# Two linear-attention layers and two memory-attention layers: stacking DMAs at slots 2 and 4, low parts taken at once, the output weight in four parts, the outer segments of the attention loop dealt anew

## The chip, the cores and the metric

The kernel runs on one core of a Trainium2 chip. The metric is the device time of one execution in microseconds. Three runs of the kernel before took 1543.25, 1537.27 and 1541.24 us, a median of 1541.24.

## What is computed

Four layers follow each other on x of 2048 tokens by 512 features, 32 heads of 16: A, B, A, B, each on a layer norm of x and added to x. A is linear attention with a learned feature map, B is causal softmax attention inside four segments of 512 tokens, mixed with a memory that sums over the segments before. The two A layers share their weights, and so do the two B layers.

```python
def _A_ref(x, wqkv, w_phi, wo):
    q, k, v = heads(x @ wqkv)
    pq, pk = q @ w_phi, k @ w_phi                      # per head
    phi = lambda p: concat([softmax(p), softmax(-p)])
    kv, z = sum_s phi(pk)^T v, sum_s phi(pk)
    return (phi(pq) @ kv / (phi(pq) @ z + 1e-6)) @ wo

def _B_ref(x, wq, wk, wv, wo, beta):
    g = sigmoid(beta)                                  # per head
    for s in range(4):                                 # segments of 512 tokens
        p = softmax(qs @ ks^T * 16**-0.5 + causal_mask)
        a_dot = p @ vs
        a_mem = phi(qs) @ M / (phi(qs) @ z + 1e-6)     # phi(t) = t + 1 if t > 0 else exp(t)
        o = g * a_mem + (1 - g) * a_dot
        M, z = M + phi(ks)^T vs, z + sum(phi(ks))
    return o @ wo

x = x + _A_ref(layernorm(x), ...); x = x + _B_ref(layernorm(x), ...)
x = x + _A_ref(layernorm(x), ...); x = x + _B_ref(layernorm(x), ...)
```

## The kernel before

Each float32 product of the projections is done as three float32r products: of an operand a high part (a copy rounded by ScalarE) and a low part (what is left, by VectorE) are made, and high x high, high x low and low x high are summed in PSUM (`mm3`, line 432). `mm3_pair` (line 447) does two such sums at once, each on one half of the rows of the array; they swap halves twice on the way, and the order at a swap is kept by a no-op on SyncE's queue (lines 458 to 462), between the last product before the swap and the first one after it.

The order of the work is written out by hand. TensorE, VectorE, ScalarE, GpSimd and SyncE each run their instructions in the order in which the program issues them (`held`, line 166; `Ordered`, line 146). All DMAs but one kind go through SyncE's queue.

The change concerns `LayerB.steps` (line 1291), the attention loop of a B layer. It has 32 units, one for each segment s (0 to 3) and each group m of four heads (eight to a segment), and five slots to a unit; k counts the slots, R = 5. In each slot the loop issues, in this order:

- one fifth of `attend` (line 1150): scores of a group into the PSUM tile `lg` (one buffer), ScalarE's exponential into `P`, GpSimd's causal mask
- one fifth of `maxima` (line 1105), which runs LEAD = 9 slots ahead: scores for the row maxima, into the PSUM tiles `mx` and `my` or, at slots 2 and 4, into two of the four `g` banks, and VectorE's masked maximum of each
- what was put off or set for this slot: `later`, `late`, and the parts and features of a projection (`projected`, line 1019: copies and splits into `ta`, features into `tb`)
- at slot STACK = 3: `stack` (line 1094), six DMAs that lay high and low parts of Q and K of a group side by side in a set `e` (`e<-ta`), for the group three units on
- at slot 0: `weighted` (line 1186), the weighted sum with the values of the unit before (`g<-P,v`), and ScalarE's scaled copy `U`
- the slot's entry in a table of text (lines 55 to 94): FIRST for segment 0, GAPS for segments 1 and 2, LAST and FINAL for segment 3 of the first and the second B layer

In the tables, "2.3" is slot 3 of unit 2 of the segment, and the words are taken from left to right by `do` (line 1305):

- `Qi/6`, `V/6`, `O/6`, `P/4`: so many steps of a pair of projections of queries and keys, of values, of the output, of the output of the last segment; a pair has 24 steps of two matmuls, so four cells of 6 make one; a + stands for the next segment
- `max`: `put_maxima` (line 1141), a transpose of the row maxima `mxs`, ScalarE's copy `mt` and a DMA from ScalarE's queue into Q's set (`e<-mt`)
- `fin`: `finish` (line 1209), four transposes of U, VectorE's division, the sum
- `ln`: one block of 128 tokens of the next segment's norm is transposed and split (`columns`, line 383); `turn` and `pt`: the same for a block of the attention's output (`turn`, line 472)
- `a0` to `a3`: half of a read of the memory (`reads`); `t0`, `m0` and so on: the transpose and the product of a write to it (`writes`)
- `n`, `N`, `load`, `begin`: a step of a norm (loads of x, moments); `w`: the load of the output weight `bwo` (`load_w`, line 224, eight DMAs of 256 KB)
- a `~` behind a word puts the low part, or the end, of that step off until after `attend` and `maxima` of the next slot (`wait`, line 133; `put_off`)

A unit without Q, V, O, v or P in its cells has no projection: units 2 and 3 of FIRST, 4, 5 and 6 of FINAL (6 has only row loads, `pre`). `opening` (line 1276) and the table BEFORE fill the slots ahead of unit 0, which run beside the last blocks of layer A.

## Time and profile before

| | |
|---|---|
| median of three runs | 1541.24 us |
| the profiled execution | 1534.9 us |
| its span, first to last instruction | 1533.1 us |
| mean granted TensorE clock | 0.974 |
| busy: TensorE, VectorE, ScalarE, GpSimd | 92%, 69%, 53%, 45% |
| first attention loop, from the first weighted sum after unit 0 to the last | 329.4 to 778.2 us |
| second attention loop, likewise | 1079.6 to 1517.9 us |

The page of the profile gives busy time, its shares in 40 slices, the DMA queues, the chain of work that ended last and the costliest groups of instructions. Other views give busy time by stretch, the instructions in order of time, and who waited for whom. PE is TensorE (PEld its weight loads), DVE VectorE, ACT ScalarE, POOL GpSimd, SP SyncE; a q behind an engine is its queue's own instructions, DMA issues among them. `g<-P,v` reads: written is tile g, read are tiles P and v. In a row of instructions stand start and length in us, engine, line, operation, tiles, shapes, count, and in brackets the engine's idle time before it with what ended it. Nearly all instructions are issued by two helpers (lines 156 and 178), so tiles tell more than lines.

### The profile page before, as it was taken

Reading aid. Unit: us, or ns where it says so; the run is one execution under the profiler, and the core shown is the slowest. Engines: PE = TensorE matmul, PEld = TensorE weight load, DVE = VectorE, ACT = ScalarE, POOL = GpSimd, SP = SyncE. Lnnn points to the kernel's source line nnn. Section 1 sums busy time; section 2 is a strip of 40 time slices with the busy share of each in tenths; the row PEclk is TensorE's granted clock in tenths of the full one; section 3 lists DMA queues with packets and bytes.
Section 4 is the critical chain, followed back from the end, with each engine's and each line's share of the span. In section 5 each row is a group of like instructions: output and inputs, shape, how many; then the busy total and the mean of one; then the engine's idle time right before and its main releaser. Section 6 shows DMA issues by size and latency. Waiting matters only on the chain.

```text
span 1533.1 us, 32910 instructions
## 1 busy us (share of the span) xinstructions
PE 1409.9 (92%) x12172; PEld 1048.0 (68%) x12172; DVE 1060.8 (69%) x3258; ACT 816.3 (53%) x1218; POOL 689.8 (45%) x1024
## 2 busy tenths in 40 slices
PE   7999988896999999999899999899789999999976
PEld 6887777663676776666568887776547767767744
DVE  5766776765687786877546677757558768777862
ACT  5554444444576576566444434553546756756643
POOL 1668753323446446334224356531325555553431
PEclk9999999997999999999899999999889999999989
DMA  5477374534444444446331006643633443433430
GB/s 182 141 282 258 111 215 134 153 100 123 119 122 122 120 124 118 122 123 173 103 124 47 31 22 193 193 151 105 173 97 92 132 139 91 132 112 91 131 85 28
DMA packets 108785, 196.01 MB, mean 128 GB/s; under 512 B 14417, under 2 KB 27857, under 8 KB 107857
## 3 DMA queue, kind: packets, MB, share of 16 engines
q1 hardware_dynamic: 107472, 193.38, 42.4%
q8 instruction: 97, 1.59, 0.4%
q10 hardware_dynamic: 1152, 0.52, 0.1%
q14 instruction: 64, 0.52, 0.1%
HBM read 101.05 MB, written 39.85 MB: 92 GB/s over the span
## 4 chain that ended last, share of the span: by engine, by line
PE 66%; DVE 13%; ACT 8%; DMA 4%; SPq 4%; issue 3%; POOL 1%; ACTq 0%; DVEq 0%; POOLq 0%
PE g L178 49%; PE lg L178 6%; PE g L182 4%; SPq L156 4%; ACT P L156 4%; PE mx L178 3%; PE lg L182 2%; DVE mx L156 2%; DVE my L156 2%; ACT U L156 1%; PE my L178 1%; DVE es L156 1%; DVE ol L156 1%; DMA w<-bwo 1%; DVE tb L156 1%
## 5 line engine op out<-in xcount | busy, mean ns | idle before, releaser
L156 ACT ACTIVATE P<-lg 128x1024 f32<-128x1024 f32 x320 | 329.2, 1029 | 197.0 <-PE lg L178 92.7
L156 POOL TENSOR_SCALAR_AFFINE_SELECT P<-P 128x256 f32<-128x256 f32 (+1 forms) x448 | 192.1, 443 | 398.7 <-ACT P L156 398.5
L156 DVE CUSTOM_DVE_ANT_0 mx<-mx,mask 128x128 f32<-128x128 f32 (+3 forms) x332 | 165.4, 498 | 73.7 <-PE my L178 56.8
L178 PE MATMUL g<-hh,wqk 64*128 64x512 f32 (+1 forms) x960 | 192.9, 399 | 11.8 <-SPq L156 9.2
L178 PE MATMUL lg<-e,e 64*128 64x256 f32 (+2 forms) x1024 | 167.9, 368 | 37.7 <-ACT P L156 37.7
L156 DVE CUSTOM_DVE_ANT_0 g<-g,mask 128x512 f32<-128x512 f32 x360 | 175.8, 544 | 23.1 <-PE g L178 21.6
L178 PE MATMUL g<-w,oh 64*128 64x512 f32 (+1 forms) x728 | 176.2, 404 | 2.2 <-ACT oh L156 0.9
L156 DVE CUSTOM_DVE_ANT_0 my<-my,mask 128x128 f32<-128x128 f32 (+3 forms) x332 | 172.6, 520 | 0.1
L178 PEld LDWEIGHTS lg<-e,e 64*128 64x128 f32 x1024 | 101.7, 194 | 92.5 <-ACT P L156 66.8
L178 PE MATMUL g<-P,v 128*32 128x512 f32 (+3 forms) x2048 | 162.0, 460 | 1.0 <-DVE mxs L156 0.8
L156 DVE DVE_READ_ACCUMULATOR2_ANT mxs<- 128x1 f32 x1024 | 145.9, 142 | 0.0
L178 PE MATMUL g<-w,hh 64*128 64x512 f32 (+1 forms) x640 | 142.4, 396 | 3.6 <-SPq L156 2.7
L178 PEld LDWEIGHTS g<-hh,wqk 64*128 64x128 f32 (+1 forms) x960 | 111.3, 187 | 32.1 <-SPq L156 11.8
L178 PEld LDWEIGHTS g<-P,v 128*32 128x32 f32 x2048 | 61.2, 115 | 96.4 <-issue 76.0
L156 ACT COPY tb<-g 128x512 f32<-128x512 f32 x144 | 81.2, 587 | 77.5 <-PE g L178 50.2
L156 POOL TENSOR_SCALAR tb<-tb 128x512 f32<-128x512 f32 x72 | 109.5, 1533 | 27.3 <-ACT tb L156 27.3
L178 PE MATMUL g<-hl,wqk 64*128 64x512 f32 (+1 forms) x480 | 113.2, 395 | 4.8 <-DVE hl L156 4.8
L178 PEld LDWEIGHTS g<-w,oh 64*128 64x128 f32 (+1 forms) x728 | 100.5, 187 | 22.1 <-issue 3.4
L178 PE MATMUL g<-w,ol 64*128 64x512 f32 (+1 forms) x364 | 113.3, 396 | 0.9 <-DVE ol L156 0.8
L178 PEld LDWEIGHTS g<-w,hh 64*128 64x128 f32 (+1 forms) x640 | 81.4, 186 | 20.9 <-SPq L156 4.6
L178 PE MATMUL mx<-e,e 63*128 63x256 f32 (+2 forms) x332 | 90.4, 336 | 3.0 <-DMA e<-ta 3.0
L156 DVE TENSOR_TENSOR ol<-g,oh 128x512 fp32r<-128x512 f32 (+1 forms) x66 | 43.8, 673 | 68.6 <-ACT oh L156 68.5
(148 smaller groups left out, 3004.4 us busy)
## 6 DMA issues: line engine op xcount, KB each, us to landing
e<-ta SPq DMA_DIRECT2D x384, 128.0 KB
wqk<-wqk SPq DMA_DIRECT2D x64, 512.0 KB
x<-x SPq DMA_DIRECT2D x48, 256.0 KB
ot<-in SPq DMA_DIRECT2D x28, 256.0 KB
pq<-tb SPq DMA_DIRECT2D x24, 256.0 KB
tb<-pq SPq DMA_DIRECT2D x24, 256.0 KB
x<-xr SPq DMA_DIRECT2D x22, 256.0 KB
xr<-x SPq DMA_DIRECT2D x20, 256.0 KB
```

The costliest lines, as they stand in the source:

```text
L156: i = f(*a, **k)
L178: return held(nc.tensor.matmul(*a, **k))
L182: return held(nc.tensor.transpose(*a))
```

## The change

`stack` takes one side at a time: Q's three DMAs are issued at slot 2 and K's three at slot 4, for the same group as before. No word of the tables has a `~` any more. In most rows `max` now stands ahead of `fin`. The load of the output weight leaves slot 1.4 of FIRST and is done in four steps (two DMAs each) at 3.2, 3.4, 4.2 and 4.4, through the generator `bring`, which `load_w` ran to its end. In FIRST the first pair of values goes from unit 5 to unit 3, the four `ln` from units 2, 3, 4, 4 to 2, 2, 3, 3, and `t1 m1` from unit 2 to 3. In FINAL Q3 goes from unit 1 to 2, the output pairs from units 2 and 3 to 3 and 5, the turns from 1, 2, 3, 3 to 1, 2, 3, 4, and one step of `a2` from unit 4 to 3. The number of instructions of each kind stays.

```diff
--- before.py
+++ after.py
@@ -32,7 +32,7 @@
 G = 4
 R = 5
 TB3 = 3
-STACK = 3
+STACK = (2, 4)
 SPARE = (2, 4)
 XR = 2
 FILL = (1, 3, 4)
@@ -54,43 +54,43 @@
 
 FIRST = """
 0.0 max            | 0.2 Q2/6          | 0.3 Q2/12         | 0.4 Q2/6
-1.0 t0 fin m0 max  | 1.1 Q3/6          | 1.2 Q3/6          | 1.3 Q3/6 | 1.4 Q3/6 w
-2.0 t1 fin ln~ m1 max
-3.0 ln~ fin max    
-4.0 ln ln~ fin max | 4.1 Q0+/6 load    | 4.2 Q0+/6         | 4.3 Q0+/6 | 4.4 Q0+/6
-5.0 t2 fin m2 max  | 5.1 V+/6          | 5.2 V+/6 n        | 5.3 V+/6 n | 5.4 V+/6
+1.0 t0 fin m0 max  | 1.1 Q3/6          | 1.2 Q3/6          | 1.3 Q3/6 | 1.4 Q3/6
+2.0 ln ln max fin
+3.0 ln ln fin t1 max m1 | 3.1 V+/6     | 3.2 V+/6 w        | 3.3 V+/6 | 3.4 V+/6 w
+4.0 max fin        | 4.1 Q0+/6 load    | 4.2 Q0+/6 w       | 4.3 Q0+/6 | 4.4 Q0+/6 w
+5.0 t2 fin m2 max  | 5.1 n             | 5.2 n
 6.0 t3 fin m3 max  | 6.1 Q1+/6         | 6.2 Q1+/6 n       | 6.3 Q1+/6 n | 6.4 Q1+/6
-7.0 a0+ a0+ fin max| 7.1 V+/6         | 7.2 V+/6 n        | 7.3 V+/6 n | 7.4 V+/6
+7.0 a0+ a0+ max fin | 7.1 V+/6         | 7.2 V+/6 n        | 7.3 V+/6 n | 7.4 V+/6
 """
 GAPS = """
-0.0 a1 a1 fin max  | 0.1 Q2/6 n        | 0.2 Q2/6 n        | 0.3 Q2/6 n | 0.4 Q2/6
-1.0 t0 turn~ fin m0 max| 1.1 Q3/6     | 1.2 Q3/6 n        | 1.3 Q3/6 | 1.4 Q3/6
-2.0 turn t1 fin ln~ m1 max| 2.1 O/6   | 2.2 O/6           | 2.3 O/6 | 2.4 O/6
-3.0 turn turn ln~ fin max| 3.1 O/6    | 3.2 O/6           | 3.3 O/6 | 3.4 O/6
-4.0 ln ln a2 fin a2 max| 4.1 Q0+/6 load | 4.2 Q0+/6       | 4.3 Q0+/6 | 4.4 Q0+/6
-5.0 t2 a3 fin m2 max| 5.1 V+/6 begin  | 5.2 V+/6 n N      | 5.3 V+/6 n N | 5.4 V+/6
-6.0 a3 t3 fin m3 max| 6.1 Q1+/6       | 6.2 Q1+/6 n N     | 6.3 Q1+/6 n N | 6.4 Q1+/6
-7.0 a0+ a0+ fin max| 7.1 V+/6         | 7.2 V+/6 n N      | 7.3 V+/6 n N | 7.4 V+/6
+0.0 a1 a1 max fin  | 0.1 Q2/6 n        | 0.2 Q2/6 n        | 0.3 Q2/6 n | 0.4 Q2/6
+1.0 t0 turn fin m0 max | 1.1 Q3/6      | 1.2 Q3/6 n        | 1.3 Q3/6 | 1.4 Q3/6
+2.0 turn t1 fin ln m1 max | 2.1 O/6    | 2.2 O/6           | 2.3 O/6 | 2.4 O/6
+3.0 turn turn fin ln max | 3.1 O/6     | 3.2 O/6           | 3.3 O/6 | 3.4 O/6
+4.0 ln ln a2 fin a2 max | 4.1 Q0+/6 load | 4.2 Q0+/6       | 4.3 Q0+/6 | 4.4 Q0+/6
+5.0 t2 a3 fin m2 max | 5.1 V+/6 begin  | 5.2 V+/6 n N      | 5.3 V+/6 n N | 5.4 V+/6
+6.0 a3 t3 fin m3 max | 6.1 Q1+/6       | 6.2 Q1+/6 n N     | 6.3 Q1+/6 n N | 6.4 Q1+/6
+7.0 a0+ a0+ max fin | 7.1 V+/6         | 7.2 V+/6 n N      | 7.3 V+/6 n N | 7.4 V+/6
 """
 LAST = """
-0.0 a1 a1 fin max  | 0.1 Q2/6 n        | 0.2 Q2/6 n        | 0.3 Q2/6 n | 0.4 Q2/6
-1.0 turn~ fin max  | 1.1 Q3/6          | 1.2 Q3/6 n        | 1.3 Q3/6 | 1.4 Q3/6
-2.0 turn fin ln~ max| 2.1 O/6         | 2.2 O/6           | 2.3 O/6 | 2.4 O/6
-3.0 turn turn ln~ fin max| 3.1 O/6    | 3.2 O/6           | 3.3 O/6 | 3.4 O/6
-4.0 ln ln a2 fin a2 max| 4.1 v/2      | 4.2 v/2           | 4.3 v/2 | 4.4 v/2
-5.0 a3 fin a3 max  | 5.1 v/2           | 5.2 v/2           | 5.3 v/2 | 5.4 v/2
-6.0 fin max        | 6.1 v/1           | 6.2 v/1           | 6.3 v/1 | 6.4 v/1 pre
-7.0 pt pt~ fin max | 7.1 P/4           | 7.2 P/5           | 7.3 P/5 | 7.4 P/4
+0.0 a1 a1 max fin  | 0.1 Q2/6 n        | 0.2 Q2/6 n        | 0.3 Q2/6 n | 0.4 Q2/6
+1.0 turn max fin   | 1.1 Q3/6          | 1.2 Q3/6 n        | 1.3 Q3/6 | 1.4 Q3/6
+2.0 turn ln fin max | 2.1 O/6          | 2.2 O/6           | 2.3 O/6 | 2.4 O/6
+3.0 turn turn fin ln max | 3.1 O/6     | 3.2 O/6           | 3.3 O/6 | 3.4 O/6
+4.0 ln ln a2 fin a2 max | 4.1 v/2      | 4.2 v/2           | 4.3 v/2 | 4.4 v/2
+5.0 a3 a3 max fin  | 5.1 v/2           | 5.2 v/2           | 5.3 v/2 | 5.4 v/2
+6.0 max fin        | 6.1 v/1           | 6.2 v/1           | 6.3 v/1 | 6.4 v/1 pre
+7.0 pt pt fin max  | 7.1 P/4           | 7.2 P/5           | 7.3 P/5 | 7.4 P/4
 """
 FINAL = """
-0.0 a1 a1 fin max  | 0.1 Q2/6          | 0.2 Q2/6          | 0.3 Q2/6 | 0.4 Q2/6
-1.0 turn~ fin max  | 1.1 Q3/6          | 1.2 Q3/6          | 1.3 Q3/6 | 1.4 Q3/6
-2.0 turn fin max   | 2.1 O/6           | 2.2 O/6           | 2.3 O/6 | 2.4 O/6
-3.0 turn turn fin max| 3.1 O/6        | 3.2 O/6           | 3.3 O/6 | 3.4 O/6
-4.0 a2 a2 fin max  
-5.0 a3 a3 fin max  
-6.0 fin max        | 6.4 pre
-7.0 pt pt~ fin max | 7.1 P/4           | 7.2 P/5           | 7.3 P/5 | 7.4 P/4
+0.0 a1 a1 max fin  | 0.1 Q2/6          | 0.2 Q2/6          | 0.3 Q2/6 | 0.4 Q2/6
+1.0 turn max fin
+2.0 turn max fin   | 2.1 Q3/6          | 2.2 Q3/6          | 2.3 Q3/6 | 2.4 Q3/6
+3.0 turn a2 max fin | 3.1 O/6          | 3.2 O/6           | 3.3 O/6 | 3.4 O/6
+4.0 turn a2 fin max
+5.0 a3 a3 max fin  | 5.1 O/6           | 5.2 O/6           | 5.3 O/6 | 5.4 O/6
+6.0 max fin        | 6.4 pre
+7.0 pt pt fin max  | 7.1 P/4           | 7.2 P/5           | 7.3 P/5 | 7.4 P/4
 """
 BEFORE = {-25: "q0 load", -23: "v0", -21: "k0",
           -18: "n", -17: "v1 n", -16: "n", -15: "n n", -14: "q1 n", -13: "n", -12: "k1 n", -11: "n", -10: "v2 n",
@@ -957,7 +957,7 @@
         def __init__(self, xsrc, xdst):
             self.xsrc, self.xdst = xsrc, xdst
             self.st, self.hT, self.vv, self.ot, self.mx, self.U = {}, {}, {}, {}, {}, {}
-            self.pr, self.at, self.k = {}, {}, BEGIN
+            self.pr, self.at, self.k, self.wo = {}, {}, BEGIN, []
             self.later, self.late, self.rows, self.turned = [], [], [], []
 
         def start(self):
@@ -1091,16 +1091,16 @@
                                in1=gates[:, 1, 8 * c : 8 * c + 8].unsqueeze(2).broadcast_to([P, 8, DH]))
             yield
 
-        def stack(self, m):
+        def stack(self, m, side):
 
             s, c, hf = m // 8, m % 8 // 2, m % 2
             d = self.st[s, c]
             d["set"] = self.sets[(s * NC + c) % NSET]
-            for t, (hi, lo), low in zip(d["set"], (d["part", 0], d["part", 1]), (2, 1)):
-                for j in range(3):
-                    part = lo if j == low else hi
-                    dma(t[j:P:4, 2 * hf : 2 * hf + 2, :].rearrange("p r x -> p (r x)"),
-                        part[64 * hf : 64 * hf + 64, :])
+            (hi, lo), low = d["part", side], 2 - side
+            for j in range(3):
+                part = lo if j == low else hi
+                dma(d["set"][side][j:P:4, 2 * hf : 2 * hf + 2, :].rearrange("p r x -> p (r x)"),
+                    part[64 * hf : 64 * hf + 64, :])
 
         def maxima(self, m):
 
@@ -1349,7 +1349,9 @@
                 elif op == "n":
                     pass
                 elif op == "w":
-                    self.wo = load_w("bwo")
+                    if not self.wo:
+                        self.wsteps = bring(self.wo, "bwo")
+                    next(self.wsteps, None)
                 elif op == "ln":
                     next(after if s == NSEG - 1 else norms[-1], None)
                 elif op == "a":
@@ -1380,9 +1382,9 @@
                 self.later, self.late = [], []
                 for f in self.at.pop(k, []):
                     f()
-                m = (k - STACK) // R + 3
-                if k % R == STACK and 0 <= m < N:
-                    self.stack(m)
+                m = k // R + 3
+                if k % R in STACK and 0 <= m < N:
+                    self.stack(m, STACK.index(k % R))
                 if k == R * N:
                     for _ in range(4):
                         next(early)
```

## The prediction

> **What bounds the kernel now.** I read the page first, then busy time by stretch, then the instructions in order of time where a stretch was longer than its work.

> ```profile
> PE 1409.9 (92%) x12172; PEld 1048.0 (68%) x12172; DVE 1060.8 (69%) x3258; ACT 816.3 (53%) x1218; POOL 689.8 (45%) x1024
> ...
> PEclk9999999997999999999899999999889999999989
> ```

> TensorE is busy for 92%, so only its idle time (123 us) and its slow clock can be won: the clock is full (9) except in a few slices. These lie in the outer segments of the two attention loops. Below, segment 0 of the first loop is cut at the first weighted product (g<-P,v) of each unit, one row for units 1 to 7 (columns: length, then busy time and count of PE, PEld, DVE, ACT, POOL, then granted clock, DMA). The next two fences are the same units of the second loop (their sum), and units 2 and 4 to 7 of that loop's last segment, with the sum of its seven.

> ```profile
> 329.43:344.02 14.59, 13.42 (x132) 9.59 (x130) 9.79 (x37) 9.06 (x14) 5.21 (x10) 1.00 0.47 128
> 344.02:362.34 18.32, 10.93 (x87) 6.82 (x85) 10.52 (x38) 9.63 (x15) 7.03 (x13) 0.72 0.74 227
> 362.34:376.48 14.14, 10.04 (x75) 5.12 (x73) 8.86 (x35) 6.50 (x9) 6.62 (x10) 0.74 0.19 43
> 376.48:395.22 18.74, 15.63 (x128) 10.65 (x126) 9.46 (x36) 7.04 (x10) 2.98 (x7) 0.84 0.36 99
> 395.22:408.87 13.65, 13.24 (x131) 9.59 (x130) 10.18 (x38) 9.84 (x16) 5.78 (x13) 1.00 0.51 137
> 408.87:422.36 13.49, 13.26 (x130) 9.65 (x130) 10.50 (x41) 7.38 (x10) 7.76 (x12) 1.00 0.27 61
> 422.36:435.11 12.75, 12.75 (x125) 9.30 (x125) 11.67 (x47) 9.33 (x16) 4.59 (x9) 1.00 0.53 146
> sum 105.68, PE 89.27 PEld 60.72 DVE 70.98 ACT 58.80 POOL 39.95; mean PE 12.75 PEld 8.67 DVE 10.14 ACT 8.40 POOL 5.71
> ```

> ```profile
> sum 105.45, PE 89.96 PEld 60.76 DVE 71.01 ACT 58.71 POOL 40.00; mean PE 12.85 PEld 8.68 DVE 10.14 ACT 8.39 POOL 5.71
> ```

> ```profile
> 1437.40:1449.82 12.42, 12.20 (x122) 8.57 (x121) 10.52 (x38) 8.97 (x14) 5.39 (x10) 1.00 0.30 67
> ...
> 1462.70:1475.37 12.67, 8.77 (x79) 5.27 (x77) 9.73 (x40) 7.00 (x10) 6.12 (x10) 0.85 0.57 168
> 1475.37:1489.47 14.10, 10.37 (x80) 5.69 (x78) 9.73 (x40) 6.08 (x8) 3.66 (x8) 0.74 0.07 20
> 1489.47:1502.86 13.39, 7.43 (x55) 3.27 (x54) 2.09 (x6) 5.82 (x7) 3.70 (x8) 0.75 0.01 2
> 1502.86:1517.93 15.07, 14.31 (x107) 8.23 (x105) 3.83 (x8) 7.43 (x10) 3.66 (x8) 0.91 0.01 1
> sum 93.57, PE 78.47 PEld 49.84 DVE 55.88 ACT 52.35 POOL 34.21; mean PE 11.21 PEld 7.12 DVE 7.98 ACT 7.48 POOL 4.89
> ```

> A unit with a projection in it (count over 120) runs at full clock in 12.4 to 13.7. One without (units 2, 3 above; 4, 5, 6 of the last segment) gives TensorE a third fewer instructions and takes as long: there ScalarE's exponentials set the pace, TensorE stands between them, and the clock falls. Three rows of granted clock in such a unit, in steps of 3.4 us:

> ```profile
> 1468.10:1471.50 3.40, 1.65 (x14) 1.01 (x14) 3.04 (x14) 1.97 (x3) 1.85 (x4) 1.00 0.88 199
> ...
> 1474.90:1478.30 3.40, 3.40 (x28) 1.14 (x28) 1.65 (x6) 1.02 (x1) 0.41 (x1) 0.50 0.00 0
> 1478.30:1481.70 3.40, 3.25 (x35) 2.10 (x27) 1.71 (x7) 0.95 (x2) 0.00 (x0) 1.00 0.10 25
> ```

> After a step that is half idle the clock is 0.50 until a whole busy step has passed, so the next unit's weighted product pays:

> ```profile
> 1462.70 2.36 PE L178 MATMUL g<-P,v 128*32 128x512 f32 x32
> ...
> 1468.77 0.56 PE L178 MATMUL lg<-e,e 64*128 64x256 f32 x4 [1.32 <-ACT P L156]
> ...
> 1475.37 3.79 PE L178 MATMUL g<-P,v 128*32 128x512 f32 x32
> ```

> That is 1.4 us, with the rest of that stretch 1.6.

> **The change part by part: the output weight.** It is now loaded at 1.4 of segment 0, eight transfers at once.

> ```profile
> 344.51 4.75 SPq L156 DMA_DIRECT2D w<-bwo  x8
> ...
> 354.16 1.02 ACT L156 ACTIVATE P<-lg 128x1024 f32<-128x1024 f32 x1 [4.54 <-DMA w<-bwo]
> ...
> 355.24 0.90 PE L178 MATMUL lg<-e,e 64*128 64x256 f32 x4 [5.20 <-ACT P L156]
> ```

> ScalarE issues a DMA of its own (the row maxima) ahead of that exponential; the profile names a landing of the weight as what it stood for. Queued behind it are the exponential and TensorE's next scores, 5.2 us, and then comes the slow clock. Loaded two transfers at a time at 3.2, 3.4, 4.2, 4.4 (SP: 4.75/8 = 0.6 each) the block should go. Bounds: no wait, or 1.3 us (a quarter of 5.2) at each of four places; I take none, since no maxima DMA is issued between two parts of one slot.

> **Segment 0 dealt anew.** Projections leave unit 5 and come to unit 3, so the unfilled units are 2 and 5, not 2 and 3. Prices of what moves:

> ```profile
> 346.31 0.66 PE L182 MATMUL g<-ident,tb 128*128 128x128 f32 x4
> 348.12 1.09 PE L178 MATMUL g<-v,tb 128*128 128x136 f32 x8
> ...
> 380.10 1.09 PE L182 MATMUL g<-ident,x 128*128 128x128 f32 x8
> ```

> Four transposes (t, turn) are 0.66, a memory write (m) 1.09, two ln steps 1.09. Unit 4's projection now finds its low parts ready from a unit earlier. Each unit by its nearest row: 1: 14.59 less a swap wait of 0.95 (below), 13.6. 2: unfilled, 12.67 with two ln for its two a steps (also 8 matmuls), 12.6. 3: 13.65 (values, t, m) + 1.09 + 1.6 of slow clock = 16.3. 4: 13.49 - 0.66 - 1.09 = 11.7, and 0.9 for a swap that stays late (four row loads and two of the weight stand ahead of it) = 12.6. 5: 12.67 with t and m for the two a, 13.2. 6: 13.49 + 1.6 = 15.1. 7: 12.75. Sum 96.1; against 105.68 and 105.45 that is 9.5 and 9.3, **19 us**. The slow clock of 1.6 is an estimate for four places, bounds 0 and 3.4 (two whole steps of 3.4 at half speed).

> [...]

> **The last loop's segment.** Unfilled units 4, 5, 6 become 1, 4, 6. By the same rows, with an a step 0.55: 1 is 12.67 with a turn for the two a, 12.2; 2 is 12.42 + 1.6 = 14.0; 3 is 12.42 + 0.55 = 13.0; 4 is 12.67 with a turn for one a, 12.8; 5 is 12.42 with two a for a turn, and 1.6, 14.5; 6 now starts at full clock, 13.39 - 1.2 = 12.2; 7 stays. That is 78.7 for units 1 to 6 against 93.57 - 15.07 = 78.5: **0.2 us lost**; three slow stretches before, three after. Bounds: 3 gained (two slow stretches less) and 6 lost (three at 3.4 for 1.6).

> **Stacking away from the swaps.** A pair of projections swaps halves at the ends of slots 1 and 3, by way of SP's queue, where the six stacking DMAs of slot 3 stand ahead of the second swap. The second fence is the row of the waits (us in total, times, longest).

> ```profile
> 336.88 4.98 SPq L156 DMA_DIRECT2D e<-ta  x6
> ...
> 341.97 0.50 PE L178 MATMUL g<-hh,wqk 64*128 64x512 f32 x2 [0.95 <-SPq L156]
> ```

> ```profile
> PE g L178 <- SPq L156: 12.5, 16, 1.5
> ```

> Three at slot 2 take 2.5 us of the two slots (2.0 each, below); three at slot 4 come behind the swap. Of 12.5 us, 2.7 are in units 1 and 4 already; of the other 9.8 I take 80%, **8 us** (bounds 0 and 9.8). What hides the K half's delay: its last DMA goes out 1.9 us after the swap and lands some 3 us later, and the next maxima that read it come a slot and a slot 0 after:

> ```profile
> 277.97 2.98 DMA e<-ta
> ```

> ```profile
> 443.36 0.46 PE L178 MATMUL lg<-e,e 64*128 64x256 f32 x4
> ...
> 445.34 0.40 PE L178 MATMUL lg<-e,e 64*128 64x256 f32 x4
> ...
> 452.97 0.28 PE L178 MATMUL mx<-e,e 63*128 63x256 f32 x1
> ```

> From slot 3 (443.36) to slot 4 (445.34) is 2.0; from slot 4 to the maxima 7.6 us, against 4.9: a margin of 2.7. Before the loop the margin is missing: the first maxima already wait 1.55 us for that landing, and K's DMAs now come behind one load of wqk (0.6): **1.2 us lost** over two loops, bounds 0 and 4.

> **Low parts at once, maxima ahead of finish.** A late low part is taken behind the next slot's maxima, and holds its PSUM bank until then, which slot 2's maxima need:

> ```profile
> 470.57 0.56 PE L178 MATMUL lg<-e,e 64*128 64x256 f32 x4
> ...
> 471.59 0.50 PE L178 MATMUL g<-e,e 63*128 63x512 f32 x1 [0.23 <-DVE hl L156]
> ...
> 473.09 0.28 PE L178 MATMUL lg<-e,e 64*128 64x256 f32 x1
> ```

> ```profile
> 468.52 0.30 DVE L156 TENSOR_TENSOR mem<-g,mem 128x136 f32<-128x136 f32 x1 [0.58 <-PE g L178]
> ```

> This slot took 2.52; the undisturbed one above 2.0. There are 18 such places outside segment 0 (three in each of four middle segments, four and two in the last ones). At 0.4 each: **7 us**. Taken at once the 0.69 us operation falls into slot 0, where VectorE idles anyway (0.58 in the row); uncovered it would cost 0.69 x 18 = 12, so bounds -12 and +13 (0.7 each). The maxima's transpose ahead of finish: nothing, it runs while TensorE waits for U; bounds -2 and +2.

> **Sum.** 19 - 0.2 + 8 - 1.2 + 7 = 32.6 us. The profiled execution took 1534.9 (span 1533.1 and 1.8 around it) and would take 1502; it lies 6.3 below the median of 1541.24, so the median should come to **1509**.

> **The rivals.** (a) VectorE becomes the bound of filled units and the freed waits reappear on it: the 8 and the 7 don't come, 1541.2 - 19 + 1.4 = 1524. For it: it is busy 11.67 of 12.75 in unit 7 above. Against: the low parts move to its idle slot 0. (b) The weight's parts still block ScalarE: 5.2 twice stays, 1519. Against: a quarter of the data at a time. (c) Other side: K's half lands after the maxima want it. It decides from a landing 2.7 us later than reckoned; each us beyond stalls some 25 filled units in each of two loops, 50 us, so from 0.65 beyond it outweighs all gains, and at 1.2 beyond it is 60 lost less 33: 1568. Against: that 2.7 margin; for: the wait at the loop's start shows it can happen. [...]

> **How the numbers follow.** Forecast 58% (alone 1498 to 1520), a 20%, b 6%, c 8%, d 8%. The low end is the forecast with no slow clock (9.6), all of the swaps (1.8) and the low parts at 13 (6), 1492, rounded to 1490; the high end is a with 6 us of its own bounds, 1530. That leaves out c and the tails, 2 in 10. A measurement here tells some 0.5% (8 us) from no change: faster 0.88 (the forecast, b, d, most of a), same 0.05 (a's tail, c at its threshold), slower 0.07 (the rest of c).

> **What would show it.** In the profile after: no idle over 2 us on TensorE in segment 0 and a granted clock of 1.00 in units 1 and 4; two slow stretches per segment 0; PE's wait for SPq under 3 us; no wait for DVE hl or ol at slot 2's maxima; VectorE's order with low parts ahead of the reciprocal. TensorE waiting for DMA e<-ta within the loop would prove c, and a loss of clock in units 3 and 6 above 3 us each would make the time too low.

## The result, and the profile after

| | runs | median, us | lowest to highest | profiled execution (span) |
|---|---|---|---|---|
| before | 4 | 1540.8 | 1537.27 to 1543.25 | 1534.9 (1533.1) |
| after | 4 | 1501.1 | 1497.69 to 1508.23 | 1500.75 (1499.0) |

The ratio is 0.975, with a 95% interval of 0.971 to 0.979. The gain is 39.7 us between medians, and 34.2 between the profiled executions, where 32.6 was forecast. The difference comes from the profiled execution of before, which lies 5.9 under its median; a possible cause stands under experiment 1.

From the page of after, busy time:

```profile
PE 1397.2 (93%) x12172; PEld 1048.4 (70%) x12172; DVE 1059.0 (71%) x3258; ACT 815.1 (54%) x1218; POOL 691.8 (46%) x1024
```

The same number of products runs. Of the 34.1 us between the two spans, 21.4 are idle time of TensorE (123.2 before, 101.8 after) and 12.7 are busy time (1409.9 to 1397.2); which the prediction had not reckoned with; why the same products are busy for less was not settled. Busy time by unit, cut like the prediction's rows (columns as there): units 1 to 7 of segment 0 in the first loop, then the sum of these units in the second loop, then the sum of units 1 to 7 of its last segment.

```profile
333.08:346.44 13.36, 13.14 (x132) 9.52 (x130) 9.80 (x37) 9.07 (x14) 3.98 (x10) 1.00 0.51 139
346.44:360.09 13.65, 9.72 (x79) 5.88 (x77) 10.70 (x38) 9.31 (x15) 7.44 (x11) 0.74 0.56 152
360.09:376.05 15.96, 15.51 (x139) 11.45 (x138) 9.91 (x37) 7.64 (x11) 7.81 (x14) 0.90 0.25 70
376.05:389.26 13.21, 11.75 (x119) 8.31 (x117) 8.41 (x34) 6.92 (x10) 2.98 (x7) 1.00 0.65 202
389.26:403.47 14.21, 10.07 (x83) 6.13 (x81) 10.70 (x40) 9.46 (x15) 5.50 (x11) 0.79 0.68 202
403.47:419.01 15.54, 15.28 (x132) 10.12 (x131) 10.02 (x41) 6.77 (x9) 7.65 (x12) 0.87 0.18 41
419.01:431.27 12.26, 12.26 (x125) 9.49 (x125) 11.47 (x46) 9.32 (x16) 4.29 (x8) 1.00 0.55 149
sum 98.19, PE 87.73 PEld 60.91 DVE 71.00 ACT 58.49 POOL 39.64; mean PE 12.53 PEld 8.70 DVE 10.14 ACT 8.36 POOL 5.66
...
sum 97.70, PE 88.28 PEld 60.62 DVE 70.67 ACT 58.60 POOL 39.74; mean PE 12.61 PEld 8.66 DVE 10.10 ACT 8.37 POOL 5.68
...
sum 92.19, PE 78.69 PEld 49.74 DVE 56.10 ACT 52.03 POOL 34.29; mean PE 11.24 PEld 7.11 DVE 8.01 ACT 7.43 POOL 4.90
```

Segment 0 is 7.5 and 7.75 us shorter (105.68 to 98.19, 105.45 to 97.70). Units 1, 4 and 7 run at clock 1.00, and no gap of TensorE is over 2 us (the longest of unit 2 is 1.79); the two slow stretches are where they were expected, over units 2 and 3 and over 5 and 6. The last segment goes from 93.57 to 92.19. TensorE's waits (us in total, times, longest):

```profile
PE lg L178 <- ACT P L156: 29.2, 29, 2.8
...
PE mx L178 <- DMA e<-ta: 7.4, 2, 3.9
...
PE g L178 <- SPq L156: 1.7, 3, 0.9
```

The wait for SP's queue fell from 12.5 to 1.7. One wait grew: the first maxima before each loop, 3.0 in both together before, 7.4 now. SP's queue there, then TensorE, then three steps of the clock (each fence one view of after):

```profile
277.71 0.33 SPq L156 DMA_DIRECT2D wqk<-wqk  x1
278.12 1.94 SPq L156 DMA_DIRECT2D e<-ta  x3
```

```profile
283.89 0.35 PE L178 MATMUL mx<-e,e 63*128 63x256 f32 x1 [3.49 <-DMA e<-ta]
```

```profile
281.30:284.70 3.40, 0.81 (x5) 0.62 (x6) 0.25 (x3) 2.33 (x4) 2.88 (x2) 1.00 0.29 93
284.70:288.10 3.40, 3.40 (x16) 2.46 (x16) 2.08 (x9) 0.19 (x1) 3.32 (x4) 0.51 0.00 0
288.10:291.50 3.40, 2.72 (x43) 2.10 (x40) 2.90 (x9) 1.94 (x3) 0.06 (x1) 0.99 0.75 205
```

K's three DMAs now come behind a load of wqk that issues in 0.33 us but carries 512 KB. The maxima wait 3.49, and a step at half clock follows. K's last transfer lands 4.15 and 4.79 us after its issue at the two entries, against 2.98 and 2.78 in before, and it is issued 1.0 us before TensorE is free for the maxima instead of 1.5.

### The profile page after: what moved, and what is told of

The parts are those of the page before. It is cut to its first block, busy times and chain, and to the rows that moved or that the text cites. A ratio compares the mean times of both kernels' runs of the same rounds, so it can differ in the third digit from the quotient of the medians.

```text
span 1499.0 us, 32930 instructions
## 1 busy us (share of the span) xinstructions
PE 1397.2 (93%) x12172; PEld 1048.4 (70%) x12172; DVE 1059.0 (71%) x3258; ACT 815.1 (54%) x1218; POOL 691.8 (46%) x1024
## 4 chain that ended last, share of the span: by engine, by line
PE 76%; DVE 8%; ACT 7%; DMA 4%; issue 2%; SPq 1%; POOL 1%; ACTq 0%; DVEq 0%; POOLq 0%
PE g L178 56%; PE lg L178 7%; PE g L182 5%; PE mx L178 4%; ACT P L156 4%; PE lg L182 2%; PE my L178 2%; DVE es L156 1%; ACT U L156 1%; SPq L156 1%; DMA wqk<-wqk 1%; DVE mx L156 1%; DVE my L156 1%; DVE tb L156 1%; DVE mmq L156 1%
## 5 line engine op out<-in xcount | busy, mean ns | idle before, releaser
L156 ACT ACTIVATE P<-lg 128x1024 f32<-128x1024 f32 x320 | 329.1, 1029 | 182.6 <-PE lg L178 99.7
L156 POOL TENSOR_SCALAR_AFFINE_SELECT P<-P 128x256 f32<-128x256 f32 (+1 forms) x448 | 192.7, 444 | 338.5 <-ACT P L156 338.3
L156 DVE CUSTOM_DVE_ANT_0 mx<-mx,mask 128x128 f32<-128x128 f32 (+3 forms) x332 | 165.5, 498 | 54.8 <-PE my L178 48.3
L178 PE MATMUL g<-hh,wqk 64*128 64x512 f32 (+1 forms) x960 | 186.5, 393 | 3.6 <-SPq L156 1.5
L156 DVE CUSTOM_DVE_ANT_0 g<-g,mask 128x512 f32<-128x512 f32 x360 | 175.9, 544 | 15.7 <-PE g L178 14.8
L178 PE MATMUL lg<-e,e 64*128 64x256 f32 (+2 forms) x1024 | 159.2, 365 | 29.6 <-ACT P L156 29.2
L156 DVE CUSTOM_DVE_ANT_0 my<-my,mask 128x128 f32<-128x128 f32 (+3 forms) x332 | 172.4, 519 | 0.0
L178 PE MATMUL g<-w,oh 64*128 64x512 f32 (+1 forms) x728 | 168.3, 403 | 1.4 <-ACT oh L156 0.9
L178 PE MATMUL g<-P,v 128*32 128x512 f32 (+3 forms) x2048 | 163.7, 464 | 1.0 <-DVE mxs L156 0.9
L178 PEld LDWEIGHTS lg<-e,e 64*128 64x128 f32 x1024 | 97.3, 193 | 81.0 <-ACT P L156 54.3
L156 DVE DVE_READ_ACCUMULATOR2_ANT mxs<- 128x1 f32 x1024 | 144.7, 141 | 0.0
L178 PE MATMUL g<-w,hh 64*128 64x512 f32 (+1 forms) x640 | 141.8, 394 | 0.6 <-DVE ol L156 0.6
L178 PEld LDWEIGHTS g<-P,v 128*32 128x32 f32 x2048 | 62.0, 115 | 96.0 <-issue 72.6
L156 POOL TENSOR_SCALAR tb<-tb 128x512 f32<-128x512 f32 x72 | 111.9, 1565 | 27.3 <-ACT tb L156 27.3
L178 PEld LDWEIGHTS g<-hh,wqk 64*128 64x128 f32 (+1 forms) x960 | 106.4, 185 | 19.7 <-SPq L156 2.5
L156 ACT COPY tb<-g 128x512 f32<-128x512 f32 x144 | 81.2, 587 | 65.6 <-PE g L178 39.6
L178 PEld LDWEIGHTS g<-w,oh 64*128 64x128 f32 (+1 forms) x728 | 92.5, 188 | 22.3 <-issue 2.9
L178 PE MATMUL g<-hl,wqk 64*128 64x512 f32 (+1 forms) x480 | 107.2, 390 | 0.4 <-DVE hl L156 0.4
L156 DVE TENSOR_TENSOR ol<-g,oh 128x512 fp32r<-128x512 f32 (+1 forms) x66 | 43.7, 672 | 86.0 <-ACT oh L156 85.9
L178 PE MATMUL g<-w,ol 64*128 64x512 f32 (+1 forms) x364 | 103.4, 398 | 0.5 <-DVE ol L156 0.5
L178 PE MATMUL mx<-e,e 63*128 63x256 f32 (+2 forms) x332 | 91.0, 338 | 7.8 <-DMA e<-ta 7.4
L178 PEld LDWEIGHTS g<-w,hh 64*128 64x128 f32 (+1 forms) x640 | 82.2, 187 | 16.0 <-issue 1.4
```

What stands on the lines that cost most here:

```text
L156: i = f(*a, **k)
L178: return held(nc.tensor.matmul(*a, **k))
```

## The experiments

All ratios are against the kernel before in runs of the same chip, with 95% intervals. There are two attention loops, so an effect in a unit of segment 0 counts twice.

**1. The stacking alone.**

```diff
 (kernel before, shortened)
-STACK = 3
+STACK = (2, 4)
-    self.stack(m)
+    self.stack(m, STACK.index(k % R))
```

> The kernel before with stacking at slots 2 and 4 alone. Theory: swaps late by the stacking DMAs are cured in the loop (TensorE's waits for SPq fall from 12.5 us to under 3, one left per loop in unit 4 of segment 0), and at each loop's entry the wait for e<-ta grows from 1.5 to 3.5 us with some 1.5 us of half clock behind it: net 2 to 6 us faster than before. Rival (the freed waits reappear on VectorE or PSUM banks): no swap waits either, but the units keep their lengths, and with the longer entry it is 5 to 8 us slower. The weight's block of 5.2 us in unit 2 of segment 0 stays in both.

Measured: 1524.31 (4 runs), ratio 0.9892 [0.9874, 0.9911], 16.6 us faster, against 8 less 1.2 in the prediction and 2 to 6 expected here. In its view of waits SP's queue is no longer listed; the wait at the loops' entry is there in full:

```profile
PE mx L178 <- DMA e<-ta: 7.7, 2, 4.0
```

Why more than the 12.5 us that the trace of before had to give? One reading is that this one execution was a mild one. The same row in experiments 2, 3 and 4, which all keep the stacking at slot 3, reads 20.9, 15.5 and 22.5 us, over 22 to 24 times. Each of them has an edit of its own, though, and no second execution of before was traced, so this is not shown. It fits that the traced execution of before lies 5.4 under the median of the 21 runs beside this experiment (1540.26) and that of experiment 2, with 20.9, lies 5.6 over its own; it would also explain why the gain between medians is larger than between profiles. Executions vary for other reasons too: of after, where the swap waits make 1.7, one took 1497.69 at a granted clock of 0.976 and one 1508.23 at 0.970.

**2. Low parts at once, alone.** Every `~` is taken out of the kernel before's tables.

```diff
-1.0 t0 turn~ fin m0 max| ...
+1.0 t0 turn fin m0 max| ...
```

> The kernel before with every low part taken at once, nothing else changed. Theory: slot 2's maxima no longer wait for a bank (no gap for DVE hl or ol at g<-e,e), 0.4 to 0.7 us in each of 18 units, and the 2.2 us wait for hl in unit 4 of segment 0 goes in both loops: 10 to 15 us faster. Rival (VectorE is the bound): the 0.69 us operation delays the maxima of slot 1 as much as it helped slot 2, within 4 us of before.

Measured: 1529.78 (6 runs), 0.9936 [0.9913, 0.9959], 9.9 us faster. TensorE's wait for the low parts, in before and then here:

```profile
PE g L178 <- DVE hl L156: 6.8, 13, 2.2
```

```profile
PE g L178 <- DVE hl L156: 0.4, 2, 0.2
```

In the first middle segment, unit 1 went from 14.11 to 13.45 and unit 2 from 15.88 to 15.15, 0.7 each, but unit 3, the third place with a late low part, from 14.86 to 14.97. So it is 0.7 at two of the three places there and nothing at the third, on average not far from the 0.4 of the prediction. Another part of the gain lies in segment 0, whose unit 4 is 1.24 and 1.44 shorter in the two loops. VectorE did not take the 0.7 of units 1 and 2 back.

**3. The order of maxima, finish and norm alone**, with the low parts still late.

```diff
-0.0 a1 a1 fin max  | ...
+0.0 a1 a1 max fin  | ...
-3.0 turn turn ln~ fin max| ...
+3.0 turn turn fin ln~ max| ...
```

> The kernel before with the maxima's transpose ahead of finish (and finish ahead of ln in unit 3), low parts still put off, old deal. By the prediction's step (it costs and brings nothing): within 2 us of before. By the reading of the trace after (units 7 and 0 of the middle segments are 0.3 to 0.5 us shorter without any other edit in them): 4 to 7 us faster.

Measured: 1536.04 (10 runs), 0.9967 [0.9953, 0.9982], 5.1 us faster. Forecast was 0, within 2. Unit 0 of the first middle segment goes from 12.64 to 12.27. TensorE's rows there, in before and then here:

```profile
438.59 0.60 PE L182 MATMUL g<-ident,U 128*128 128x128 f32 x4
439.02 0.27 PE L182 MATMUL g<-ident,mxs 128*16 128x128 f32 x1
```

```profile
439.77 0.27 PE L182 MATMUL g<-ident,mxs 128*16 128x128 f32 x1
439.88 0.60 PE L182 MATMUL g<-ident,U 128*128 128x128 f32 x4
```

The maxima's transpose had stood between U's transposes and the next scores, and now runs ahead of U's. Five of the six such units are 0.2 to 0.4 shorter, 1.5 in all (the sixth is 0.3 longer); the unfilled units 4, 5 and 6 of the last segment of the second loop, which have the same edit, give about another 1.5. Unit 7 of that middle segment has it too and stays at 12.81, and the filled units of the last segments show no steady change. Where the rest comes from was not settled, since the swap waits, 15.5 here, are others in this execution.

**4. Segment 0 and the weight in four parts alone**, stacking still at slot 3 (only the table FIRST and the operation `w` are those of after).

> The kernel before with the new table of segment 0 and the output weight in four parts, the rest as before (stacking at slot 3, put-off parts elsewhere). Theory: units 1 to 7 of segment 0 take 98 to 100 us for 105.6, 12 to 16 us faster over two loops, with two stretches of half clock to a segment. Rival (the block moves with the load): a wait of TensorE over 2 us for ACT P in units 3 to 5 and less than 5 us gained.

Measured: 1536.64 (10 runs), 0.9976 [0.9963, 0.9989], 3.7 us faster: a miss. The weight's block is gone, but units 1 to 7 take 102.16 and 101.63 in the two loops for the 98 to 100 expected, and unit 4 of the first takes 16.93. SP's queue, then TensorE:

```profile
381.53 1.75 SPq L156 DMA_DIRECT2D x<-x  x4
383.33 0.90 SPq L156 DMA_DIRECT2D w<-bwo  x2
384.32 4.58 SPq L156 DMA_DIRECT2D e<-ta  x6
```

```profile
389.02 0.80 PE L178 MATMUL g<-hh,wqk 64*128 64x512 f32 x2 [3.23 <-SPq L156]
```

Twelve transfers stand ahead of the swap. In this program, the records of the trace carry, for each DMA, the semaphore that it raises when it has landed and those that are waited for ahead of it. The same stretch in these terms:

```
issue us   transfer  raises  waits for
382.90     x<-x      101
386.84     e<-ta     100     100
388.38     e<-ta     101     101 (raised by the x<-x of 382.90, landed 388.37)
388.96     the swap's mark on SP's queue
```

The DMAs of SP and ScalarE take turns over eight such semaphores, and a transfer that comes to a semaphore here waits until the one that had it before has landed. So the last stacking DMA stood 0.9 us for the landing of a row load issued eight transfers earlier, and the swap stood behind it. How late the swap is here hangs on when a load lands; whether such waits vary by that from execution to execution was not shown.

**5. Stacking, segment 0 and four parts together**, without the rest.

> The kernel before with stacking at slots 2 and 4, the new table of segment 0 and the output weight in four parts; the other segments as before. Theory (the new segment 0 gained only 7.3 us alone because row loads, weight parts and six stacking DMAs together made the swaps of units 3 and 4 late): units 3 and 4 take 16 and 13 to 13.5 us, segment 0 from unit 1 on 98 to 99 us, and the kernel is 26 to 34 us faster than before, more than the 16 and 4 of the two edits alone. Rival (the two edits add): about 20 us faster.

Measured: 1513.39 (4 runs), 0.9813 [0.9792, 0.9833], 28.8 us faster, where 16.6 and 3.7 alone make 20.3. Unit 4 and the sum of segment 0:

```profile
376.62:389.87 13.25, 11.76 (x119) 8.30 (x117) 8.41 (x34) 6.92 (x10) 2.98 (x7) 1.00 0.66 199
...
sum 98.56, PE 87.97 PEld 60.85 DVE 70.79 ACT 58.55 POOL 39.64; mean PE 12.57 PEld 8.69 DVE 10.11 ACT 8.36 POOL 5.66
```

Unit 4 is 13.25, not 16.93: the new segment 0 crowds SP's queue ahead of its swaps, and pays only with the stacking split. With 9.9 and 5.1 for experiments 2 and 3 the parts make 43.8, against 39.7 for the whole, so these do not simply add.

**6. All eight parts of the weight at once, in after.**

```diff
-                    if not self.wo:
-                        self.wsteps = bring(self.wo, "bwo")
-                    next(self.wsteps, None)
+                    if not self.wo:
+                        self.wo = load_w("bwo")
```

> The changed kernel with all eight transfers of the output weight at 3.2 of segment 0 instead of two at each of four slots. Theory (ScalarE's own DMA stands for a landing of the weight when many transfers are ahead of it): the block comes back in unit 4, where the next row maxima are sent, 2 to 5 us of TensorE's wait in each loop and slow clock behind it: 5 to 14 us slower than the changed kernel. Rival (what helped was the later place, not the parts): unit 4 within 0.5 us of the changed kernel.

Measured: 1514.72 (one run), 13.6 above after's median. ScalarE's own DMA was not held up: it is issued at 381.79, right behind the copy `mt`, which ends at 381.76. Instead SP's queue and TensorE show:

```profile
372.41 3.93 SPq L156 DMA_DIRECT2D w<-bwo  x8
376.51 2.29 SPq L156 DMA_DIRECT2D e<-ta  x3
```

```profile
376.45 0.73 PE L178 MATMUL g<-w,hh 64*128 64x512 f32 x4 [1.71 <-SPq L156]
...
385.22 0.55 PE L178 MATMUL mx<-e,e 63*128 63x256 f32 x1 [2.48 <-DMA e<-ta]
```

The swap is late behind eight issues, and K's half of the stack is late for the maxima: rival c at one place, brought about by a queue that is full ahead of K. Units 3 and 4 of the first loop take 17.92 and 17.43, against 15.96 and 13.21 in after.

**7. K of the first group stacked one slot earlier, ahead of the load of wqk, in after.**

```diff
+                if k == -12:
+                    self.stack(0, 1)
-                if k % R in STACK and 0 <= m < N:
+                elif k % R in STACK and 0 <= m < N and k != -11:
```

> The changed kernel with one difference: of the first group alone K's three stacking DMAs are issued one slot earlier, ahead of the load of wqk. Theory: the wait for e<-ta at each loop's entry falls from 3.5 to 3.9 us back to about 1.5 and the half clock behind it goes: 6 to 9 us faster than the changed kernel, about 1493 us. Rival (the landing is late for the parts of K, or the bandwidth): entry within 1 us of the changed kernel.

Measured: 1494.84 (4 runs), 0.9705 [0.9691, 0.9719], 6.3 us faster than after by medians. The two intervals overlap, but all four runs here (to 1495.89) lie below all four of after (from 1497.69). SP's queue, and the wait:

```profile
276.51 4.17 SPq L156 DMA_DIRECT2D e<-ta  x6
280.78 0.62 SPq L156 DMA_DIRECT2D wqk<-wqk  x1
```

```profile
PE mx L178 <- DMA e<-ta: 3.4, 2, 1.7
```

4.0 of the 6.3 are the wait itself (7.4 to 3.4). K's last transfer now lands 3.25 and 3.16 us after its issue, and it is issued 1.6 us before TensorE is free. The half-clock step behind each wait, worth up to 1.7 (half of its 3.41), is gone as well; TensorE's rows with their clock in these places, two steps at the first entry and two at the second:

```profile
279.01:282.43 3.42, 2.50 (x12) 1.73 (x10) 0.95 (x2) 2.72 (x5) 0.55 (x2) 1.00 0.96 259
282.43:285.84 3.41, 2.62 (x16) 1.99 (x18) 2.06 (x9) 2.32 (x5) 2.90 (x2) 1.00 0.47 148
1006.05:1009.47 3.42, 1.69 (x10) 1.08 (x8) 0.69 (x1) 3.39 (x7) 0.69 (x1) 1.00 0.93 275
1009.47:1012.88 3.41, 3.41 (x36) 2.52 (x36) 2.87 (x10) 2.30 (x4) 3.33 (x3) 1.00 0.06 25
```

**8. The last segment as it was dealt before, in after** (table FINAL of before, with the low parts at once and the maxima first).

> The changed kernel with the old deal of the last segment of the second loop (unfilled units 4, 5, 6; low parts at once and maxima ahead of finish kept). By the prediction (0.2 us lost by the new deal): the segment from unit 1 on within 2 us of the changed kernel's 92.2. By the reading after (1.4 us gained, part of it from the order): 0 to 2 us longer.

Measured: 1499.47 (one run); units 1 to 7:

```profile
sum 91.91, PE 78.23 PEld 50.82 DVE 55.66 ACT 51.93 POOL 34.10; mean PE 11.18 PEld 7.26 DVE 7.95 ACT 7.42 POOL 4.87
```

0.28 less than after, in one execution of each: the new deal of that segment is worth about nothing, as forecast.

**9. Segment 0's unfilled units filled, in after.** Units 2 and 5 get 12 products of one weight tile with another a slot (`d`) in slots 1 to 4, whose results nobody reads.

```diff
-2.0 ln ln max fin
+2.0 ln ln max fin  | 2.1 d | 2.2 d | 2.3 d | 2.4 d
-5.0 t2 fin m2 max  | 5.1 n             | 5.2 n
+5.0 t2 fin m2 max  | 5.1 d n | 5.2 d n | 5.3 d | 5.4 d
```

> The changed kernel with 96 products of the value weight with itself added in the unfilled units 2 and 5 of segment 0, 12 in each of slots 1 to 4; their results are not read. Theory (the clock falls because those units leave TensorE half idle): granted clock 1.00 in units 2, 3, 5 and 6, units 3 and 6 1.5 to 2.3 us shorter each, units 2 and 5 within 1 us of 13.5: added work makes it 3 to 9 us faster over two loops. Rival (the slow clock comes from something else, or costs little): units 2 and 5 longer by 2 us or more and 3 and 6 as before, 4 to 10 us slower.

Measured: 1495.54 (4 runs), 0.971 [0.9685, 0.9735], 5.6 us faster than after by medians, with work added. The intervals overlap (after's is 0.971 to 0.979); units 1 to 7 of segment 0 carry the reading, 3.3 and 2.7 us shorter in the two loops. Units 2, 3 and 6 of the first loop, and the sum of seven:

```profile
346.93:360.12 13.19, 12.50 (x128) 9.64 (x126) 10.59 (x38) 9.14 (x15) 7.12 (x11) 1.00 0.55 158
360.12:374.59 14.47, 14.02 (x139) 10.71 (x138) 9.91 (x37) 7.82 (x11) 8.13 (x14) 1.00 0.27 72
...
402.66:416.14 13.48, 13.25 (x129) 9.62 (x130) 9.76 (x39) 5.98 (x8) 7.24 (x12) 1.00 0.21 47
...
sum 94.87, PE 90.26 PEld 66.83 DVE 70.89 ACT 58.56 POOL 39.66; mean PE 12.89 PEld 9.55 DVE 10.13 ACT 8.37 POOL 5.67
```

The clock stays at 1.00 in all of these units. Unit 2, with 48 products more, is not longer (13.65 before the filling); units 3 and 6 lose 1.5 and 2.1 us. What the filling takes away in unit 2 are three gaps of 0.64 to 0.75 us and all but 0.69 of one of 1.79, so gaps no longer than these were enough for the clock to fall in after.

**10. Both: entry and filling**, the last segment's units 1, 4 and 6 filled too (unread products again).

> The changed kernel with the K half of the first group stacked ahead of wqk and unread products in all unfilled units: 2 and 5 of segment 0 in both loops, 1, 4 and 6 of the last segment of the second loop. Theory: the clock is 1.00 there too and units 2, 5 and 7 of the last segment lose 1.5, 1 and 1.4 us; with 6 us each from the entry and segment 0 it comes to 1481 to 1489 us. Rival (in the last segment the added work costs what the clock gives): 1488 to 1492.

Measured: 1485.81 (4 runs), 0.9628 [0.9605, 0.9651]. The last segment's sum goes from 92.19 to

```profile
sum 86.38, PE 84.78 PEld 60.44 DVE 56.44 ACT 52.06 POOL 34.33; mean PE 12.11 PEld 8.63 DVE 8.06 ACT 7.44 POOL 4.90
```

though TensorE is busy for 6.1 us more in it (78.69 to 84.78).

**11. Real work as filling**: experiment 7 with unit 6's pair of projections spread over units 5 and 6 (`Q1+/6` in unit 6 becomes `Q1+/3` in both), nothing unread.

> The changed kernel with the first group's K stacked earlier (as e6_entry) and, in segment 0, the pair Q1 spread over units 5 and 6, 3 steps in each of eight slots instead of 6 in four; no work added. Theory: no unfilled unit 5, the clock stays at 1.00 in units 5 and 6, which together take 26.5 to 28.5 us for 29.7: 2 to 6 us faster than e6_entry. Rival (two PSUM banks held through slot 0 of unit 6 make finish, t3 and m3 wait): units 5 and 6 together 29 us or more.

Measured: 1491.85 (4 runs), 0.9671 [0.9646, 0.9697], not told apart from experiment 7. Units 5 and 6 of the first loop:

```profile
386.89:402.35 15.46, 11.90 (x108) 7.67 (x106) 11.30 (x40) 10.24 (x15) 6.37 (x11) 1.00 0.75 219
402.35:415.69 13.34, 11.42 (x106) 7.26 (x106) 9.76 (x39) 6.74 (x10) 6.87 (x12) 1.00 0.19 39
```

The clock holds, but TensorE idles 3.6 of 15.46 in unit 5, and both units together take 28.8 against 29.75 in after. In the second loop they take 30.3, with clock 0.90 in unit 5: what the clock gives, new waits take (in the first loop 1.2 us for a load of `wqk` and 1.5 for the row maxima). The 26.5 to 28.5 expected for the two units were missed.

**12. Experiment 10 with the load of awk taken in four steps** in the last segment of the first loop, where unit 6 has a wait of 2.8 for ScalarE.

```diff
-                wk = load_w("awk", None, "e8")
+                wk = []
+                wks = bring(wk, "awk", None, "e8")
+                next(wks)
                 for n, _ in enumerate(vt):
+                    next(wks, None)
```

> As e9_fill_all, and the load of awk at the end of the first loop in four steps of two DMAs instead of eight at once. Theory (there too ScalarE's row-maxima DMA stands behind eight transfers, 2.7 us at unit 6): that wait falls under 1 us and unit 6 of the last segment of the first loop takes 12 to 13.5 us for 14 to 15.5: 1 to 4 us faster than e9_fill_all. Rival (the wait is for something else): unit 6 unchanged.

Measured: 1481.45 (4 runs), 0.961 [0.959, 0.9631], the fastest median of all, though its interval overlaps that of experiment 10. The wait did not go, and unit 6 takes 15.36, against 13.49 in experiment 10. SP's queue, then ScalarE:

```profile
724.50 3.74 SPq L156 DMA_DIRECT2D e<-awk  x8
```

```profile
730.05 0.25 ACT L156 ACTIVATE mt<-g 16x128 fp32r<-16x128 f32 x1
733.09 0.53 ACTq L156 DMA_DIRECT2D e<-mt  x1
733.72 1.02 ACT L156 ACTIVATE P<-lg 128x1024 f32<-128x1024 f32 x1 [3.41 <-DMA e<-awk]
```

The eight still go out in one run, so the load was not spread in time and the edit settles nothing about spreading. The semaphores name what ScalarE's DMA stands for, here and at the weight in before:

```
kernel          issue us  transfer  raises  waits for
experiment 12   726.30    e<-awk    104     104
                733.09    e<-mt     104     104 (its wait ends at 733.03)
before          346.61    w<-bwo    99      99
                353.60    e<-mt     99      99  (its wait ends at 353.54)
```

It needs nothing of that data. It takes the next turn of the eight, and so waits for the landing of a load issued 6.8 and 7.0 us earlier. ScalarE had finished the copy `mt` at 730.30 and, in before, at 349.63: it stood 2.7 and 3.9 us.

## Why the prediction was right, and where it was off

The time (1509 forecast, 1501.1 measured) and its direction came out, and mostly for the reasons given; for the profiled execution 1502 was reckoned and 1500.75 measured. To that the prediction added the 6.3 us by which before's profiled execution lay under its median; after's lies at its median. By the terms of the sum:

- **Segment 0, 19.** By the traces 7.5 and 7.75, together 15.2. Units 2 and 5 take 13.65 and 14.21 where 12.6 and 13.2 were reckoned. The slow clock carried into units 3 and 6 was sized well (15.96 and 15.54 against 16.3 and 15.1). The weight's block went, so b falls; unit 4 took 13.2 against 12.6. Not foreseen: this gain needs the split stacking (experiments 4 and 5).
- **The last segment, -0.2.** About nothing (experiment 8).
- **Swaps, 8.** The mechanism held, waits of SP's queue 12.5 to 1.7, but the term was too small: the stacking alone, with the dearer entry in it, brought 16.6. That the size was taken from one mild execution is likely (15.5 to 22.5 in three other traces with the stacking at slot 3), but not shown.
- **Entry, -1.2.** The term too small: about -6.3 for two loops by experiment 7. The prediction priced the load of wqk ahead of K's DMAs by its issue (0.6), which is about right (they are issued 0.5 later), but not by the 512 KB that pass ahead of them: the last of them takes 1.2 and 2.0 us longer from issue to landing. And it took no loss of clock behind the wait. Even the bound of 4 was passed.
- **Low parts, 7.** 9.9 measured, of which 1.24 and 1.44 in the traces are unit 4 of segment 0, which the prediction has under segment 0. In the middle segments the average of 0.4 a place was about right, made of up to 0.7 at two places and nothing at a third. VectorE did not take the gain back, so a falls.
- **Maxima ahead of finish, 0 within 2.** 5.1 measured (interval 2.8 to 7.2, 1540.3 times 0.0018 and 0.0047), beyond its bounds: the prediction held that the transpose runs while TensorE waits for U, but in unit 0 it stood between U's transposes and the scores. That explains a part; some 2 us stay open.

The misses have both signs and cancel in part. Stacking with its entry brought 16.6 where 6.8 was reckoned, segment 0 on top of it 12.2 (experiment 5) for 19, low parts 9.9 for 7, the order 5.1 for 0: in all 43.8 for 32.6, and 39.7 for the whole change. That the forecast of the time came so close is partly luck. Rival c did not come about in after: the only waits for e<-ta are the two at the entries. Experiment 6 shows that it does where the queue is filled.

Rival d, that no clock is lost behind the unfilled units (9.6 less), does not hold: in after the granted clock is 0.74 and 0.90 over units 2 and 3 and 0.79 and 0.87 over units 5 and 6 of segment 0 in the first loop. Unread products in units 2 and 5, whose gaps in after are at most 1.79 us, kept it at 1.00 and made segment 0 3.3 and 2.7 us shorter (experiment 9). The clock of after also fell behind a step with no gap over 0.65 us (last section).

## What to carry to other kernels

An order that is carried through a DMA queue cost here what stood ahead in that queue: TensorE's waits for it came to 12.5 to 22.5 us in four traces with the stacking at slot 3 and to 1.7 in after, and a load that had yet to land was part of it (0.9 us in experiment 4). Size such a wait from several executions where it may vary, and look where the queue is crowded before moving work to it. Where another engine's pace left TensorE half idle, filling it paid here, even with unread products (1501.1 to 1485.81 with the entry mended). A DMA put behind a load of 512 KB was late by more than that load's issue: 0.5 us of issue and 1.2 to 2.0 us of later landing.

## What the hardware showed that was not expected

```profile
1124.41:1127.83 3.42, 1.76 (x12) 0.83 (x12) 2.25 (x10) 2.55 (x4) 1.22 (x3) 1.00 0.68 261
1127.83:1131.24 3.41, 2.44 (x16) 1.97 (x16) 3.38 (x13) 2.43 (x5) 1.75 (x5) 0.50 0.77 181
```

In the third row of experiment 7, with 1.69 us busy and a gap of 1.73, the clock stayed; why it did there is open.
- DMAs of SP and ScalarE share eight semaphores in turn in this program, and so a transfer waited 2.7 us (730.30 to 733.03 in experiment 12) and 3.9 us (349.63 to 353.54 in before) for the landing of one that has nothing to do with it.
